# Moving 66 element-wise instructions of a Fourier and gated-MLP kernel from POOL to VectorE

## Chip, core and metric

One core of a Trainium2 chip runs the whole program. The metric is the device time of one execution in microseconds. PE is the matrix engine (TensorE), DVE is VectorE, ACT is ScalarE, POOL is GpSimd and SP the engine that issues the loads; each engine works through a queue of its own.

## What is computed

Three layers follow each other on 4 batches of 768 tokens with 384 channels, all in float32 at the inputs and outputs:

```
state = state + beta * outer(k_n, v - state^T k_n)   # 8 heads of 48, token by token
x  = concat of the heads' q @ state                  # [4, 768, 384]
u  = x + real(fft(fft(x, tokens), channels))
x2 = u + relu(norm(u) @ w_ch1) @ w_ch2               # 384 -> 1536 -> 384
h  = relu(x2 @ w_in)                                 # 384 -> 1024 = (hu, hv)
out = (hu * (w_spatial @ norm(hv) + b_spatial)) @ w_out
```

## The kernel before

**Attention (up to about 318 us).** The recurrence is done in chunks of 64 tokens, 12 chunks for each batch, four batches staggered. In each iteration PE runs four small stages; DVE subtracts, masks and scales (L384, L357); ACT copies out of the matmul banks. The order on every engine is written out by hand here: `chain()` ties each instruction behind the one before it on its engine. In the last 11 iterations other work is mixed in: the Fourier transform of batch 0 (`dft`) and the first five weight pieces (`conv2` in `tail()`).

**Fourier transform (`dft`).** One generator for each batch. Real input lets it fold the tokens on DVE (L575 to L586), form sums and differences of three parts (L591 to L596), then multiply by cosine and sine tables on PE (L603 to L609, L625), and add the result to x (L635 to L647). Batch 0 runs inside the attention, batches 1 to 3 inside the first MLP. In batch 0 the four additions into x are on DVE, in batches 1 to 3 on POOL.

**Weight pieces (`conv2`).** A matrix product of float32 quality is made of three passes in a reduced format: high by high, high by low, low by high (`PASS`). Each weight is therefore split into a high and a low part. For a piece of 128 by 384 (w1, w2, w_out) or 128 by 512 (w_in) the chain is: ACT scales the upper word (L678), DVE masks and merges the two 32-bit words of the 64-bit input in three instructions (L680, L681, L684), ACT rounds the result to the high part (L690), and POOL subtracts it from the result, which gives the low part (L691). The w_spatial pieces are float32 already and need only the ACT and the POOL step. The staging tile `cvd` has three buffers, which come free when the low part is written. There are 24 pieces of w1 and w2, 10 of w_in and w_out, 12 of w_spatial.

**First MLP (`mlp1`, about 316 to 682 us).** Eight groups of 384 tokens; in each, 12 blocks of hidden channels. For a block PE does nine matmuls (L760), ACT takes the relu as high part `hh` (L765), DVE makes the low part `hl` (L766), and one block later PE does nine matmuls into the three outputs (L775). In group 0 the weights of a block are converted just ahead of its use. The norm and transpose of the next group (L727 to L740, L716, L717) and the Fourier work of batches 1 to 3 are mixed in, then the pieces of w_in and w_out. From here on the order on each engine isn't written by hand: a planner sets it, from assumed costs of the instructions and the engine that each is given, in program order among those ready.

**Second MLP (`mlp2`, from about 682 us).** For each batch: values and their norm (L829 to L846), gates (L854, L861), the mix over tokens (L868) and the output (L888). The 12 pieces of w_spatial are converted during batch 0. POOL makes the low parts of the values (L846) and of the gated product (L879).

Of the kernel before, what the change touches and what calls it, by code (L numbers as in the profile page):

```python
# [7 lines left out]
F32 = mybir.dt.float32  # L8
# [50 lines left out]
class Kernel:  # L59
# [509 lines left out]
    def dft(self, b, x, p):  # L569
        nc, sc, dc, sg = self.nc, self.sc, self.dc, self.sg  # L570
        X = x[b]
        ff = p(0, [128, 3, 388])
        for t in range(3):
            xs = p(3, [128, 2, DM])
            nc.vector.tensor_add(xs[:, 0], X[:, t], X[:, 3 + t])  # L575
            nc.vector.tensor_sub(xs[:, 1], X[:, t], X[:, 3 + t])
            f = p(6, [128, DM])
            nc.vector.tensor_copy(out=f[:, 0:193:192], in_=xs[:, 0, 0:193:192])
            nc.vector.tensor_add(f[:, 1:192], xs[:, 0, 1:192], xs[:, 0, 383:192:-1])
            nc.vector.tensor_sub(f[:, 193:384], xs[:, 1, 1:192], xs[:, 1, 383:192:-1])  # L580
            h = ff[:, t]
            nc.vector.tensor_copy(out=h[:, 96:289:192], in_=f[:, 96:289:192])
            nc.vector.tensor_add(h[:, 0:96], f[:, 0:96], f[:, 192:96:-1])
            nc.vector.tensor_sub(h[:, 97:193], f[:, 0:96], f[:, 192:96:-1])
            nc.vector.tensor_add(h[:, 193:288], f[:, 193:288], f[:, 383:288:-1])
            nc.vector.tensor_sub(h[:, 289:384], f[:, 193:288], f[:, 383:288:-1])  # L586
            yield
        e0, e1, e2 = (ff[:, t, :DM] for t in range(3))
        ab = p(1, [128, 3, DM])
        sm, r3, c15 = (ab[:, t] for t in range(3))  # L590
        nc.gpsimd.tensor_add(sm, e1, e2)  # L591
        nc.vector.tensor_sub(e1, e1, e2)
        nc.gpsimd.tensor_add(e2, e0, sm)
        nc.vector.scalar_tensor_tensor(out=r3, in0=e0, scalar=sg[:, 0:1], in1=e1, op0=MUL, op1=SUB)
        nc.vector.scalar_tensor_tensor(out=c15, in0=e0, scalar=sg[:, 1:2], in1=e1, op0=MUL, op1=ADD)
        nc.vector.scalar_tensor_tensor(out=e0, in0=e0, scalar=2.0, in1=sm, op0=MUL, op1=SUB)  # L596
        yield
        z = []
        for g, (a0, a1) in enumerate(MG):
            m, o, n0 = a1 - a0, (0 if g < 2 else 641), (65 if g < 2 else 64)  # L600
            pz = self.bank("pf", [128, 512])
            zv = pz[:m, :384].rearrange("p (k r) -> p r k", r=6)
            nc.tensor.matmul(pz[:m, 0 : 6 * n0 : 6], lhsT=e2[:, a0:a1], rhs=sc[:, o : o + n0], start=True, stop=True)  # L603
            o += n0
            nc.tensor.matmul(zv[:, 3], lhsT=r3[:, a0:a1], rhs=sc[:, o : o + 64], start=True, stop=True)
            o += 64
            for r, w in ((slice(1, 6, 4), (c15, sm)), (slice(2, 5, 2), (e0, e1))):
                for i in range(2):
                    nc.tensor.matmul(zv[:, r], lhsT=w[i][:, a0:a1], rhs=sc[:, o : o + 128], start=(i == 0), stop=(i == 1))  # L609
                    o += 128  # L610
            if g % 2 == 0:
                z2 = p(4 + g // 2, [97, 2, 386])
            zz = z2[:, g % 2]
            n = 385 if g < 2 else 384
            nc.scalar.copy(out=zz[:m, :n], in_=pz[:m, :n])
            z.append(zz)
            yield
        A = p(0, [128, 3, 388]).rearrange("p t (a l) -> p t a l", a=2)

        def dst(out, k0, k1, gs):  # L620
            for g in gs:
                m = MG[g][1] - MG[g][0]
                lo, n = ((0, 97), (1, 96), (1, 96), (0, 97))[g]
                o = (0, 97, 193, 289)[g]
                nc.tensor.matmul(  # L625
                    out[:, lo : lo + 2 * n - 1 : 2], lhsT=z[g][:m, k0:k1], rhs=dc[:m, o : o + n], start=True, stop=True
                )

        for t in range(3):
            pf = self.bank("pf", [128, 2, 256])  # L630
            dst(pf[:, 1], 128 * t, 128 * t + 128, (2, 3))
            dst(pf[:, 0], 128 * t, 128 * t + 128, (0, 1))
            q = p(7, [128, 194])
            nc.scalar.copy(out=q[:, :193], in_=pf[:, 1, :193])
            nc.vector.tensor_sub(A[:, t, 0, :193], pf[:, 0, :193], q[:, :193])  # L635
            nc.vector.tensor_add(A[:, t, 1, :193], pf[:, 0, :193], q[:, :193])
            yield
        pf = self.bank("pf", [128, 2, 256])
        dst(pf[:1, 0], 384, 385, (0, 1))
        sv = p(8, [1, DM])  # L640
        nc.vector.tensor_add(sv[:, :193], X[0:1, 3, :193], pf[0:1, 0, :193])
        nc.vector.tensor_add(sv[:, 193:], X[0:1, 3, 193:], pf[0:1, 0, 191:0:-1])
        for e, lo in ((0, 0), (1, 1)):
            Y = X[:, 3 * e : 3 * e + 3]
            eng = nc.gpsimd if b else nc.vector
            eng.tensor_add(Y[:, :, :193], Y[:, :, :193], A[:, :, lo, :193])
            eng.tensor_add(Y[:, :, 193:], Y[:, :, 193:], A[:, :, 1 - lo, 191:0:-1])  # L647
        nc.gpsimd.tensor_copy(out=X[0:1, 3], in_=sv)
        self.mixed.add(b)
        yield  # L650

# [14 lines left out]
    def conv2(self, stg, w):  # L666

        nc = self.nc
        _, _, raw, src, n, new = w
        d = stg.tile([128, CK], F32, name="cvd", bufs=CF["cvd"])[:, :n]  # L670
        if raw is None:
            self.load(out=d, in_=src)
        else:
            r = raw.rearrange("p (n t) -> p n t", t=2)
            e = stg.tile([128, CK], I32, name="cve", bufs=CF["cve"])[:, :n]
            di = d.bitcast(I32)

            nc.scalar.activation(d, r[:, :, 1].bitcast(F32), AF.Abs, scale=2.0**-112)  # L678
            yield
            nc.vector.tensor_single_scalar(out=e, in_=r[:, :, 1], scalar=-(2**31), op=ALU.bitwise_and)  # L680
            nc.vector.scalar_tensor_tensor(  # L681
                out=di, in0=di, scalar=3, in1=e, op0=ALU.logical_shift_left, op1=ALU.bitwise_or
            )
            nc.vector.scalar_tensor_tensor(  # L684
                out=di, in0=r[:, :, 0], scalar=29, in1=di, op0=ALU.logical_shift_right, op1=ALU.bitwise_or
            )
        yield
        t = new(F32R)
        w[:2] = t[:, 0], t[:, 1]
        nc.scalar.copy(out=t[:, 0], in_=d)  # L690
        nc.gpsimd.tensor_sub(t[:, 1], d, t[:, 0].bitcast(F32))  # L691

    def weight(self, p, name, n, first=None):

# [431 lines left out]
```

## Time and profile before

| | |
|---|---|
| median of 3 runs | 945.8 us (944.82 to 946.86) |
| the profiled execution | 946.22 us, its span in the trace 944.4 us |
| PE busy | 890.4 us, 94% of the span |
| DVE busy | 580.0 us, 61% |
| ACT busy | 405.8 us, 43% |
| POOL busy | 155.1 us, 16%, 145 instructions |
| mean granted clock of PE | 0.969 of full speed |

The span runs from the first instruction to the last in the trace; the time of an execution holds a little more around it. A busy share is an average over stages with different limits, so it says little by itself: a stage is read from the stretch of the trace that holds it. The number before an arrow is what waits, the one behind it what released it.

### The profile page before, as it was taken

What the parts mean: (1) busy time and instruction counts of PE and PEld (TensorE: products, weight loads), DVE (VectorE), ACT (ScalarE), POOL (GpSimd) and SP (SyncE); (2) the same over time, 40 slices, a digit from 0 to 9 for tenths busy, and PEclk for the clock granted to TensorE, in tenths of its full rate; (3) what the DMA queues carried; (4) which work ended last, traced back from release to release, by engine and by line L of the source; (5) the groups of instructions that cost most, each with busy time, mean ns of one, the idle gap of its engine ahead of it and who ended that gap; (6) DMA issues with size and microseconds to landing.
All of it is one profiled execution on the core that took longest, in us unless ns stands there. A gap on an engine that the chain in (4) does not pass through costs nothing.

```text
span 944.4 us, 18349 instructions
## 1 busy us (share of the span) xinstructions
PE 890.4 (94%) x7232; PEld 846.2 (90%) x7232; DVE 580.0 (61%) x1678; ACT 405.8 (43%) x1030; POOL 155.1 (16%) x145
## 2 busy tenths in 40 slices
PE   7979899999898859999999999999999999999998
PEld 7569889988898748999998999999989999899898
DVE  5999999998876999375469422322372442533521
ACT  3367878898955435222225111111251342332421
POOL 2000000000001245212126000000072132132221
PEclk8968998999999879999999999999999999999999
DMA  8666576733262620000150000000020000000001
GB/s 237 174 177 167 145 185 183 191 104 86 78 190 68 236 83 1 1 1 1 40 163 0 1 1 1 1 1 17 26 76 26 26 1 26 26 1 26 26 1 51
DMA packets 51160, 67.13 MB, mean 71 GB/s; under 512 B 28897, under 2 KB 41410, under 8 KB 51074
## 3 DMA queue, kind: packets, MB, share of 16 engines
q1 hardware_dynamic: 51074, 65.96, 24.4%
q8 instruction: 57, 0.93, 0.4%
q14 instruction: 29, 0.24, 0.1%
HBM read 61.22 MB, written 4.72 MB: 70 GB/s over the span
## 4 chain that ended last, share of the span: by engine, by line
PE 66%; DVE 23%; ACT 4%; issue 2%; DMA 2%; POOL 2%; ACTq 0%; SPq 0%; POOLq 0%; DVEq 0%
PE bankY L775 13%; PE bankX L760 12%; PE bankX L868 11%; PE bankY L888 5%; PE bankX L854 5%; PE bankX L829 4%; DVE tm L273 4%; DVE Ts L278 4%; DVE cvd L681 2%; PE bankY L383 2%; PE bankY L367 2%; PE bankY L398 2%; PE bankY L396 2%; PE bankX L198 2%; PE bankX L609 2%
## 5 line engine op out<-in xcount | busy, mean ns | idle before, releaser
L760 PE MATMUL bankX<-uh,w 128*128 128x384 f32 x576 | 165.1, 348 | 12.6 <-ACT w L690 9.1
L775 PE MATMUL bankY<-w,hh 128*128 128x384 f32 x576 | 136.4, 343 | 1.2 <-ACT hh L765 0.4
L766 DVE SCALAR_TENSOR_TENSOR hl<-bankX,hh 128x384 fp32r<-128x384 f32 x96 | 52.9, 554 | 129.2 <-ACT hh L765 120.6
L765 ACT ACTIVATE hh<-bankX 128x384 fp32r<-128x384 f32 x96 | 46.6, 491 | 176.6 <-PE bankX L760 168.1
L760 PEld LDWEIGHTS bankX<-uh,w 128*128 128x128 f32 x576 | 106.5, 191 | 16.8 <-ACT w L690 11.1
L775 PEld LDWEIGHTS bankY<-w,hh 128*128 128x128 f32 x576 | 104.1, 190 | 4.2 <-POOL w L691 1.8
L868 PE MATMUL bankX<-ws,vh 128*128 128x384 f32 x384 | 98.6, 337 | 0.0
L760 PE MATMUL bankX<-ul,w 128*128 128x384 f32 x288 | 98.3, 341 | 0.0
L775 PE MATMUL bankY<-w,hl 128*128 128x384 f32 x288 | 83.6, 342 | 2.4 <-DVE hl L766 2.3
L876 DVE TENSOR_TENSOR g<-bankX,bsb 128x384 f32<-128x384 f32 x32 | 17.8, 557 | 102.0 <-PE bankX L868 102.0
L398 PE MATMUL bankY<-Sb,cw 112*112 112x96 f32 (+1 forms) x352 | 65.5, 269 | 11.3 <-DVE cw L384 8.9
L396 PE MATMUL bankY<-WU,gak 128*112 128x96 f32 (+1 forms) x384 | 69.6, 270 | 0.3
L868 PEld LDWEIGHTS bankX<-ws,vh 128*128 128x128 f32 x384 | 69.1, 188 | 0.0
L868 PE MATMUL bankX<-ws,vl 128*128 128x384 f32 x192 | 64.3, 337 | 0.0
L398 PEld LDWEIGHTS bankY<-Sb,cw 112*112 112x112 f32 (+1 forms) x352 | 49.4, 179 | 13.1 <-DVE cw L384 7.6
L278 DVE TENSOR_TENSOR Ts<-Ts,tm 128x110 f32<-128x110 f32 (+26 forms) x264 | 59.0, 261 | 0.8
L273 DVE TENSOR_TENSOR tm<-Ts 128x110 f32<-128x110 f32 (+26 forms) x264 | 58.9, 260 | 0.9
L367 PE MATMUL bankY<-gak,TT 128*128 128x96 f32 x384 | 55.2, 290 | 3.7 <-issue 3.1
L775 PEld LDWEIGHTS bankY<-w,hl 128*128 128x128 f32 x288 | 52.9, 189 | 4.4 <-DVE hl L766 4.3
L760 PEld LDWEIGHTS bankX<-ul,w 128*128 128x128 f32 x288 | 55.0, 191 | 0.2 <-DVE ul L717 0.2
L367 PEld LDWEIGHTS bankY<-gak,TT 128*128 128x128 f32 x384 | 49.9, 203 | 5.7 <-issue 3.3
L396 PEld LDWEIGHTS bankY<-WU,gak 128*112 128x112 f32 (+1 forms) x384 | 53.6, 182 | 1.0 <-ACT x L413 0.6
(168 smaller groups left out, 1853.1 us busy)
## 6 DMA issues: line engine op xcount, KB each, us to landing
kq<-in_kq_dram SPq DMA_DIRECT2D x40, 448.0 KB, 4.3
qt<-in_qt_dram SPq DMA_DIRECT2D x48, 196.0 KB, 3.7
gak<-in_kv_dram SPq DMA_DIRECT2D x48, 192.0 KB, 3.9
w<-in_w_dram SPq DMA_DIRECT2D x24, 384.0 KB, 7.3
out_dram<-ot SPq DMA_DIRECT2D x24, 192.0 KB, 2.0
kn<-in_kn_dram SPq DMA_DIRECT2D x16, 192.0 KB, 4.6
s<-in_wi_dram SPq DMA_DIRECT2D x6, 512.0 KB, 4.0
cvd<-in_ws_dram SPq DMA_DIRECT2D x12, 192.0 KB, 2.4
```

Of the source, the lines that this page charges most:

```text
L273: nc.vector.tensor_tensor(out=tm, in0=T[:, r, k : k + 1].to_broadcast(sh), in1=T[:, k : k + 1, :k].to_broadcast(sh), op=MUL)
L278: nc.vector.tensor_add(o, o, tm)
L367: nc.tensor.matmul(pb[:, hp].rearrange("p t d -> p (t d)"), lhsT=tt[:, o + hp], rhs=kv[:, hp], start=True, stop=True)
L396: nc.tensor.matmul(pd[:m, hp], lhsT=ak[:, hp, :m], rhs=u[:, hp], start=True, stop=(c == 0))
L398: nc.tensor.matmul(pd[:m, hp], lhsT=cw[:, hp, :m], rhs=sb[:, hp], start=False, stop=True)
L760: nc.tensor.matmul(ph, lhsT=w1[f][i][:, c * 128 : c * 128 + 128], rhs=cur[k][:, c], start=(c + j == 0), stop=(c == 2 and j == 2))
L765: nc.scalar.activation(hh, ph, AF.Relu)
L766: nc.vector.scalar_tensor_tensor(out=hl, in0=ph, scalar=0.0, in1=hh.bitcast(F32), op0=MAX, op1=SUB)
L775: nc.tensor.matmul(acc[t], lhsT=hx[i][:, t * 128 : t * 128 + 128], rhs=w2[e][k], start=(e == 0 and j == 0), stop=(e == 11 and j == 2),)
L854: nc.tensor.matmul(pu, lhsT=wi[2 * c][i][:, f * 128 : f * 128 + 128], rhs=xT[hf][k][:, c], start=(c + j == 0), stop=(c == 2 and j == 2),)
L868: nc.tensor.matmul(pv, lhsT=vn[i][:, s, f * 128 : f * 128 + 128], rhs=ws[2 * s + hf][k], start=(s + j == 0), stop=(s == 5 and j == 2),)
L888: nc.tensor.matmul(po, lhsT=gt[i][:, f, t * 128 : t * 128 + 128], rhs=wo[f][k], start=(f + j == 0), stop=(f == 3 and j == 2),)
```

## The change

The low parts of all weights (46 instructions), the sums of the Fourier transform (8 instructions, L591 and L593 for four batches), its additions into x for batches 1 to 3 (12 instructions) and its copy of one row into x (4 instructions) go from POOL to DVE. That the 4 additions of batch 0 were on DVE already leaves 66 instructions with 128 partitions and 4 one-row copies that move. POOL keeps the memsets, L846 and L879.

```
@@ dft
-        nc.gpsimd.tensor_add(sm, e1, e2)
+        nc.vector.tensor_add(sm, e1, e2)
         nc.vector.tensor_sub(e1, e1, e2)
-        nc.gpsimd.tensor_add(e2, e0, sm)
+        nc.vector.tensor_add(e2, e0, sm)
...
         for e, lo in ((0, 0), (1, 1)):
             Y = X[:, 3 * e : 3 * e + 3]
-            eng = nc.gpsimd if b else nc.vector
-            eng.tensor_add(Y[:, :, :193], Y[:, :, :193], A[:, :, lo, :193])
-            eng.tensor_add(Y[:, :, 193:], Y[:, :, 193:], A[:, :, 1 - lo, 191:0:-1])
-        nc.gpsimd.tensor_copy(out=X[0:1, 3], in_=sv)
+            nc.vector.tensor_add(Y[:, :, :193], Y[:, :, :193], A[:, :, lo, :193])
+            nc.vector.tensor_add(Y[:, :, 193:], Y[:, :, 193:], A[:, :, 1 - lo, 191:0:-1])
+        nc.vector.tensor_copy(out=X[0:1, 3], in_=sv)
@@ conv2
         nc.scalar.copy(out=t[:, 0], in_=d)
-        nc.gpsimd.tensor_sub(t[:, 1], d, t[:, 0].bitcast(F32))
+        nc.vector.tensor_sub(t[:, 1], d, t[:, 0].bitcast(F32))
```

## Rows read from the trace of the kernel before

**Rows 1.** The chain that ended last, shares of the span by engine.

```profile
PE 66%; DVE 23%; ACT 4%; issue 2%; DMA 2%; POOL 2%; ACTq 0%; SPq 0%; POOLq 0%; DVEq 0%
```

**Rows 2.** Busy time by stretch: length, PE, PEld, DVE, ACT, POOL, clock, DMA, GB/s.

```profile
296.00:318.00 22.00, 17.78 (x132) 16.52 (x132) 20.07 (x44) 12.28 (x31) 4.52 (x5) 0.84 0.13 30
318.00:345.00 27.00, 19.84 (x85) 15.73 (x85) 27.00 (x75) 10.14 (x21) 12.26 (x9) 0.91 0.66 254
345.00:378.00 33.00, 25.99 (x123) 22.51 (x123) 31.03 (x53) 14.97 (x32) 15.74 (x14) 0.87 0.00 1
378.00:480.00 102.00, 100.64 (x663) 99.31 (x662) 53.64 (x170) 23.15 (x54) 16.94 (x15) 1.00 0.06 20
480.00:520.00 40.00, 37.94 (x222) 36.35 (x221) 35.62 (x70) 18.16 (x37) 20.40 (x15) 1.00 0.22 70
...
680.00:712.00 32.00, 30.99 (x161) 27.93 (x161) 22.60 (x62) 17.43 (x42) 20.12 (x18) 1.00 0.19 56
```

**Rows 3.** Waits of PE, 318 to 378 us: total us, times, longest.

```profile
PE bankX L760 <- ACT w L690: 9.1, 6, 3.1
PE bankX L760 <- POOL w L691: 3.4, 3, 1.7
```

**Rows 4.** POOL's groups, 296 to 378 us: busy us, mean ns, idle before.

```profile
L691 POOL TENSOR_TENSOR w<-cvd,w 128x384 fp32r<-128x384 f32 x24 | 28.8, 1205 | 58.9 <-ACT w L690 47.2 <-DMA w<-in_w_dram 11.7
```

**Rows 5.** DVE's groups, 296 to 378 us.

```profile
L681 DVE SCALAR_TENSOR_TENSOR cvd<-cvd,cve 128x384 int32<-128x384 int32 x23 | 19.2, 840 | 1.8 <-ACT cvd L678 1.5
L684 DVE SCALAR_TENSOR_TENSOR cvd<-w,cvd 128x384 int32<-128x384 int32 x23 | 14.9, 648 | 0.2
L680 DVE TENSOR_SCALAR cve<-w 128x384 int32<-128x384 int32 x23 | 11.0, 477 | 0.0
L766 DVE SCALAR_TENSOR_TENSOR hl<-bankX,hh 128x384 fp32r<-128x384 f32 x11 | 6.0, 545 | 0.0
...
L717 DVE TENSOR_TENSOR ul<-bankX,uh 128x384 fp32r<-128x384 f32 x5 | 2.7, 548 | 0.4 <-ACT uh L716 0.4
...
L711 DVE TENSOR_SCALAR l1v<-l1v 128x3 f32<-128x3 f32 x2 | 1.9, 931 | 0.0
...
L578 DVE COPY s<-s 128x2 f32<-128x2 f32 x4 | 1.8, 439 | 0.0
```

**Rows 6.** Single lines over the whole span: ns min/median/max, first and last start.

```profile
L681 DVE SCALAR_TENSOR_TENSOR cvd<-cvd,cve x34: 544/560/1789, 289.0 to 516.5; 128x384 int32<-128x384 int32 x28, 128x512 int32<-128x512 int32 x6
L684 DVE SCALAR_TENSOR_TENSOR cvd<-w,cvd x24: 530/552/1386, 289.6 to 376.6; 128x384 int32<-128x384 int32 x24
L680 DVE TENSOR_SCALAR cve<-w x24: 326/348/1194, 288.5 to 372.3; 128x384 int32<-128x384 int32 x24
L711 DVE TENSOR_SCALAR l1v<-l1v x8: 129/168/991, 309.8 to 526.1; 128x3 f32<-128x3 f32 x8
L578 DVE COPY s<-s x12: 146/159/996, 264.9 to 450.7; 128x2 f32<-128x2 f32 x12
```

**Rows 7.** DVE in order of time: start, us, line.

```profile
325.43 0.55 DVE L576 TENSOR_TENSOR s<-x 128x384 f32<-128x384 f32 x1
325.90 0.55 DVE L684 SCALAR_TENSOR_TENSOR cvd<-w,cvd 128x384 int32<-128x384 int32 x1
```

**Rows 8.** ACT's copies to the high part: ns min/median/max, first and last start.

```profile
L690 ACT CAST w<-cvd x24: 494/512/517, 296.4 to 377.2; 128x384 fp32r<-128x384 f32 x24
```

**Rows 9.** Waits, 385 to 480 us.

```profile
PE bankX L603 <- POOL s L593: 1.4, 1, 1.4
```

**Rows 10.** Waits, 480 to 522 us.

```profile
PE bankY L775 <- DVE hl L766: 2.0, 2, 1.6
```

**Rows 11.** The additions into x on either engine: ns min/median/max.

```profile
L646 POOL TENSOR_TENSOR x<-x,s x6: 1202/1315/1443, 396.7 to 486.8; 128x579 f32<-128x579 f32 x6
L646 DVE TENSOR_TENSOR x<-x,s x2: 744/745/746, 300.6 to 302.0; 128x579 f32<-128x579 f32 x2
```

## The prediction

> **What bounds the kernel now.** I read the chain of waits first, to see which engines set the end: PE holds 66% of it, DVE 23%, POOL 2% [rows 1]. So POOL's own time is hardly on the path, and DVE's is. Then I cut the span into stretches around the instructions that move [rows 2]. Three kinds of stage show. From 296 to 378 us DVE is the bound: 20.07 of 22 us, 27.00 of 27 and 31.03 of 33, while PE is busy for 17.78, 19.84 and 25.99 us. This is the end of attention and group 0 of the first MLP, where each weight must be converted before its matmuls. From 378 us on PE is full (100.64 of 102, 37.94 of 40, 30.99 of 32) and DVE has slack, except from 480 to 520 us, where it is busy for 35.62 of 40 us with the pieces of w_in and w_out. Before 296 us nothing but one pair of Fourier sums is touched.
>
> The waits of PE from 318 to 378 us say what the first stage lacks: 9.1 us for ACT's high parts and 3.4 us for POOL's low parts [rows 3]. ACT is busy for 10.14 of 27 and 14.97 of 33 us [rows 2], so it isn't slow; it waits for DVE, which feeds it. What shortens DVE's work between 296 and 378 us shortens the kernel, and what lengthens it there lengthens the kernel.
>
> **What POOL costs DVE now.** The 24 low parts take POOL 28.8 us, 1.205 us each [rows 4], beside the work of DVE. It isn't free. In the same stretch lines of DVE take longer than they usually do: L681 has a mean of 840 ns against a median of 560 over the whole span, L684 648 against 552, L680 477 against 348, and tiny ones stretch most: L711, on 3 elements, 931 against 168, L578, on 2 elements, 439 against 159 [rows 5, 6]. The lines that read one operand from a matmul bank, L766 and L717, keep 545 and 548 ns [rows 5]. So an instruction of DVE that works on SBUF alone is held while POOL works, and others aren't. The time lost, mean less median, by count: L681 23 x 0.28 = 6.4 us, L684 23 x 0.096 = 2.2, L680 23 x 0.129 = 3.0, L711 2 x 0.763 = 1.5, L578 4 x 0.28 = 1.1. Three more small lines (L580, L709, L710) repeat L711's pattern, one long use of about 0.8 us each, 2.4 in all. That makes 16.6 us over 27 instructions of POOL, 0.61 us each. And once DVE stands idle for 1.5 us before L681, until ACT has written a staging tile [rows 5]; ACT waited there for the tile to come free, that is for POOL.
>
> **What the same work costs on DVE.** The trace has no low part of a weight on DVE, but L717 and L766 are the same subtraction with the same result type, at 545 to 548 ns, and L576 with both inputs in SBUF takes 0.55 us [rows 5, 7]. In a full queue the next instruction starts earlier: L576 starts at 325.43 and L684 behind it at 325.90, so each takes 0.47 us of the queue [rows 7]. Between 296 and 378 us there come 24 low parts, two Fourier sums of batch 1 and one copy of a row. At 0.47 us the 26 are 12.2 us; for the copy I take 0.3, between L578's 0.16 and the 0.47. Together 12.5 us.
>
> Balance on DVE in this stretch: -16.6 - 1.5 + 12.5 = -5.6 us. Bounds: if the stretching had another cause and stayed, +12.5 - 1.5 = +11, which would be a slower kernel and is counted with the first rival below; that the waits of 3-element lines grow fivefold only beside POOL speaks against it. If the low parts fill gaps as well, -7.
>
> **The wait that is added.** A low part needs ACT's high part, a copy of 0.512 us [rows 8], and now DVE itself stands in line for it, with the next piece, `hl` and the norm queued behind. From below the cost is nothing, if other work stands between L684 and the subtraction; from above it is 24 x 0.51 = 12.2 us. The nearest rows are L717 and L766, which wait for ACT in just this way: 0.4 us over 16 instructions, 0.025 each [rows 5]. I take that: 24 x 0.025 = +0.6. The order is set by a planner that puts an instruction in the queue when its inputs should be there, which speaks for the low end; in the attention's last iterations (4 of the 24) the order is written out, and ACT's copy stands just ahead of the subtraction in the same step.
>
> **The other places.**
> - Fourier sums of batch 2: PE waits 1.4 us for L593 [rows 9], which takes POOL 1.3. On DVE it is 0.55, so I take -0.8 (bounds -1.4 and 0). The other batches' sums are waited for by nobody on PE.
> - Pieces of w_in and w_out, 480 to 520 us: PE loses 2.0 us to `hl` behind DVE's full queue [rows 10]. By the same 0.61 us, the 10 low parts cost DVE 6.1 us now and 6 x 0.6 + 4 x 0.47 = 5.5 then, where 0.6 is 0.47 scaled by 512/384. Little changes: I take -0.5 (bounds -2 and +1).
> - Additions into x, batches 1 to 3: 1.315 us on POOL, 0.745 on DVE [rows 11]. Four in a row now hold DVE for 3.0 us, with `hl` behind them, while PE is full [rows 2] and no cover is left if `hl` is late. PE has another block's nine matmuls between, so I take +0.5 (bounds 0 and +3, one microsecond for each batch). The loads into the slots of the last batch's tables start 2 us earlier, which nothing waits for.
> - w_spatial, 680 to 712 us: 12 x 0.47 = 5.6 us on a DVE that is idle for 9.4 of 32 [rows 2], against 12 x 0.61 = 7.3 of stretching gone. PE loses 1.0 us there now. I take 0 (bounds -1 and +1).
> - Batch 0's sums, before 296 us: DVE has room there and PE is not held by them; 0.
>
> **Sum.** -5.6 + 0.6 - 0.8 - 0.5 + 0.5 = -5.8 us. The profiled execution took 946.2 us for a span of 944.4, so it would be 940.4; against the median of 945.8, 0.4 lower, the forecast is **940.0 us**. Its own range is 937 to 943.5.
>
> **Rivals.**
> - *DVE waits for ACT (slower).* In its single queue DVE stands before each low part until the copy is through. What speaks for it: all 24 pieces run L684, copy, subtraction, and no independent work is promised between. Against it: 0.025 us for each of 16 like instructions. It decides from 5.6 / 24 = 0.23 us per low part on; fully exposed it is 12.2 - 5.6 = +6.6, or 952.4. Chance 0.16.
> - *A new order (no change).* The planner plans with other engines and may put PE's blocks in another order after 378 us, where PE is full and every hole shows. Three holes of the size of [rows 9, 10], 1.5 us each, give back 4.5 of 5.8: 944.5. That the gain has no place to go otherwise speaks against it. Chance 0.14.
> - *No overlap on DVE.* A subtraction released by a semaphore may take its whole 0.55 us instead of 0.47: 26 x 0.08 = 2.1 us less gain, 942.1. [Rows 7] speak against it in a full queue. Chance 0.10. The Trainium skill has this as a rule (VectorE: DVE Perf Modes, The DRAIN you can't avoid): the next instruction starts only when the pipeline of the one before is empty. By the same page (The TRN2 errata) an estimate is (384 + 151) / 0.96 = 557 ns each, with which the sum would be -3.5 us; the trace agrees on the duration and not on the spacing.
> - *PE no longer waits for weights.* Both waits of [rows 3] go, 12.5 us, and 0.8 of the Fourier sums: 932.5. DVE would have to shed twice what I count. Chance 0.10.
>
> **Numbers.** The forecast has 0.50. Faster by over 0.2% (1.9 us, about what a measurement of this kernel can tell from no change): forecast, no overlap and no waits, 0.70. Same 0.14, slower 0.16. Range 932 to 948.5: it takes in all but the far end of the first rival and the tail below the last, some 0.15.
>
> **What would show it.** Right: L681, L684, L680, L711 near their medians between 296 and 378 us; L691 on DVE at 0.55 us; the last w piece some 5 us earlier; less waiting of L760. Wrong: idle time of DVE before L691 released by L690 above 0.23 us each; the stretching still there without POOL; new holes of PE after group 0, at L775 for `hl` or at L603.

## The result and the profile after

The changed kernel takes 937.02 us (median, 936.13 to 937.29), beside 946.33 us of the kernel before on the same chip: a ratio of 0.9905 [0.9894, 0.9917]. So it is faster, as forecast, and inside the range of 932 to 948.5, but the gain of 9.3 us is 1.6 times the forecast 5.8. The profiled execution took 936.92 us for a span of 935.1. Behind L645 every line number is now one lower: the high part is L689, the low part L690, the matmuls of the first MLP L759 and L774.

First the page, its busy times and the shares of the chain that ended last:

```profile
PE 884.8 (95%) x7232; PEld 842.7 (90%) x7232; DVE 579.9 (62%) x1748; ACT 405.3 (43%) x1030; POOL 70.3 (8%) x75
...
PE 72%; DVE 20%; ACT 5%; issue 2%; DMA 1%; POOL 0%; ACTq 0%; DVEq 0%; POOLq 0%
```

DVE was given 70 instructions and is busy for 579.9 us, where it was 580.0 before. What it took over it got back by working faster. PE's share of the chain went from 66% [rows 1] to 72%, DVE's from 23% to 20%.

The same stretches as in [rows 2]; the one from 345 us is also cut where the weights now end, at 372:

```profile
296.00:318.00 22.00, 16.54 (x122) 14.96 (x122) 19.41 (x49) 12.04 (x30) 0.00 (x0) 0.84 0.16 43
318.00:345.00 27.00, 19.11 (x88) 15.45 (x86) 27.00 (x87) 9.63 (x21) 0.00 (x0) 0.94 0.63 244
...
345.00:378.00 33.00, 30.78 (x165) 28.37 (x166) 28.38 (x66) 16.82 (x36) 0.00 (x0) 0.90 0.00 0
372.00:378.00 6.00, 6.00 (x38) 5.96 (x37) 1.55 (x4) 1.46 (x3) 0.00 (x0) 1.00 0.00 0
378.00:480.00 102.00, 99.62 (x653) 98.14 (x653) 60.96 (x194) 22.18 (x53) 0.00 (x0) 1.00 0.08 25
480.00:520.00 40.00, 40.00 (x234) 39.62 (x233) 36.17 (x90) 17.94 (x37) 0.00 (x0) 1.00 0.18 57
680.00:712.00 32.00, 32.00 (x175) 30.41 (x174) 18.39 (x65) 15.01 (x34) 10.80 (x9) 1.00 0.14 43
```

From 318 to 345 us DVE is still full, but it gets through 87 instructions where it got through 75. From 372 us on it is nearly free and PE is full: group 0 ends some 6 us earlier. In the two later stretches PE, which lost 2.06 us of 40 and 1.01 of 32, now loses nothing. Only from 378 to 480 us is PE worse off: 99.62 us where it had 100.64.

DVE's groups from 296 to 378 us, against [rows 5, 6]:

```profile
L690 DVE TENSOR_TENSOR w<-cvd,w 128x384 fp32r<-128x384 f32 x24 | 12.9, 550 | 0.2 <-ACT w L689 0.2
L683 DVE SCALAR_TENSOR_TENSOR cvd<-w,cvd 128x384 int32<-128x384 int32 x23 | 12.7, 551 | 0.1
L680 DVE SCALAR_TENSOR_TENSOR cvd<-cvd,cve 128x384 int32<-128x384 int32 x23 | 12.4, 550 | 0.1
L679 DVE TENSOR_SCALAR cve<-w 128x384 int32<-128x384 int32 x23 | 8.1, 352 | 0.0
...
L578 DVE COPY s<-s 128x2 f32<-128x2 f32 x4 | 0.6, 150 | 0.0
...
L710 DVE TENSOR_SCALAR l1v<-l1v 128x3 f32<-128x3 f32 x2 | 0.3, 165 | 0.0
```

Every mean is at the median that the line had over the whole span before. The 840 ns are 550, the 931 ns of three elements are 165. And the 24 low parts made DVE wait for ACT for 0.2 us in all. Their end, in DVE's order of time (start, us, line):

```profile
370.55 0.55 DVE L683 SCALAR_TENSOR_TENSOR cvd<-w,cvd 128x384 int32<-128x384 int32 x1
371.01 0.55 DVE L690 TENSOR_TENSOR w<-cvd,w 128x384 fp32r<-128x384 f32 x1
371.73 0.56 DVE L690 TENSOR_TENSOR w<-cvd,w 128x384 fp32r<-128x384 f32 x1 [0.17 <-ACT w L689]
```

A low part starts 0.46 us behind the instruction ahead of it, though each lasts 0.55. The last one starts at 371.73 us; on POOL it started at 377.81:

```profile
377.81 1.02 POOL L691 TENSOR_TENSOR w<-cvd,w 128x384 fp32r<-128x384 f32 x1 [1.69 <-ACT w L690]
```

PE's waits from 318 to 378 us, and then those from 378 us to the end:

```profile
PE bankX L759 <- ACT w L689: 4.7, 4, 1.9
PE bankX L759 <- DVE w L690: 3.6, 2, 1.9
PE bankY L774 <- DVE w L690: 1.5, 1, 1.5
PE bankY L774 <- ACT w L689: 0.2, 1, 0.2
```

```profile
PE bankX L739 <- DVE un L731: 2.4, 1, 2.4
```

Of the 12.5 us that L760 waited [rows 3] its successor L759 still waits 8.3, and L774 waits 1.7: this stage is still bound by the weights. The waits of [rows 9, 10] are gone, and a new one has come, for the norm `un`.

To place the 9.3 us, the start of the n-th matmul of the changed kernel is compared with that of the kernel before (7232 in each trace, one profiled execution of each). The table gives the change in that difference over five parts of the span, in us; the times are those of the kernel before. It also holds the kernels of the next section.

```
                     0-283   283-409   409-497   497-543   691-720   whole
changed kernel       -0.84     -5.09     +0.94     -2.95     -1.35    -9.27
w1w2_only            -0.97     -5.98      0.00     +0.47     -0.04    -6.51
win_wout_only        -1.74     +0.03     -0.02     -2.97     +0.02    -4.69
wspatial_only        -1.03     +1.13      0.00     +0.04     -1.28    -1.14
fourier_only         -1.17     -2.48     +2.51     -1.33     +0.05    -2.42
weights_only         -0.42     -6.26     -0.01     -2.98     -1.30   -10.97
weights_only_again   -0.96     -6.25     -0.02     -2.98     -1.45   -11.66
additions_on_pool    -1.51     -6.36     +1.20     -2.98     -1.43   -11.08
sums_on_pool         -0.59     -4.29     +3.69     -2.91     -1.40    -5.48
all_on_vector        -0.71     -5.08     +0.94     -2.95     -1.50    -9.26
ghost_read           -0.51     +4.06     +2.56     -1.96     -1.25    +2.92
ghost_write          -1.00     -4.90     +2.41     -2.91     -1.28    -7.66
```

Before 283 us nothing differs but batch 0's pair of Fourier sums, and all 12 gain 0.4 to 1.7 us there, those that leave the sums alone too: the profiled execution of the kernel before was slow in its attention. That is a spread of single executions and no effect of the change; `wspatial_only` has 1.13 us more in a stretch where it differs in nothing. What is under some 1.2 us in this table is read only where it repeats.

A part of this spread is PE's granted clock. From 283 to 409 us it stood at half (1.2 of 2.4 GHz) for 20.5 us in the kernel before, for 17.1 in the changed kernel and in all kernels that move the pieces of w1 and w2 and give POOL no useless work, for 27.3 in `wspatial_only` and for only 10.2 in `fourier_only`. So the -2.48 of `fourier_only` isn't read as an effect of its edit. How much of the other gains the 3.4 us less at half hold, at most about 1.7 (an estimate: half of 3.4), was not separated.

### The profile page after: what moved, and what is told of

It reads as the page before. It is cut to its first block, busy times and chain, and to the rows that moved or that the text cites. A ratio compares the mean times of both kernels' runs of the same rounds, so it can differ in the third digit from the quotient of the medians.

```text
span 935.1 us, 18282 instructions
## 1 busy us (share of the span) xinstructions
PE 884.8 (95%) x7232; PEld 842.7 (90%) x7232; DVE 579.9 (62%) x1748; ACT 405.3 (43%) x1030; POOL 70.3 (8%) x75
## 4 chain that ended last, share of the span: by engine, by line
PE 72%; DVE 20%; ACT 5%; issue 2%; DMA 1%; POOL 0%; ACTq 0%; DVEq 0%; POOLq 0%
PE bankX L759 14%; PE bankY L774 14%; PE bankX L867 11%; PE bankX L853 5%; PE bankX L828 5%; PE bankY L887 5%; DVE tm L273 4%; DVE Ts L278 4%; PE bankY L383 2%; PE bankY L367 2%; PE bankY L396 2%; PE bankY L398 2%; PE bankX L609 2%; PE bankX L198 1%; DVE cw L384 1%
## 5 line engine op out<-in xcount | busy, mean ns | idle before, releaser
L759 PE MATMUL bankX<-uh,w 128*128 128x384 f32 x576 | 163.9, 347 | 8.3 <-ACT w L689 4.7
L774 PE MATMUL bankY<-w,hh 128*128 128x384 f32 x576 | 136.6, 343 | 1.8 <-DVE w L690 1.5
L759 PEld LDWEIGHTS bankX<-uh,w 128*128 128x128 f32 x576 | 106.5, 191 | 12.1 <-ACT w L689 6.4
L774 PEld LDWEIGHTS bankY<-w,hh 128*128 128x128 f32 x576 | 103.6, 190 | 4.2 <-DVE w L690 2.3
L759 PE MATMUL bankX<-ul,w 128*128 128x384 f32 x288 | 97.9, 340 | 0.0
L774 PE MATMUL bankY<-w,hl 128*128 128x384 f32 x288 | 82.2, 340 | 0.0
L845 POOL TENSOR_TENSOR vl<-v,vh 128x512 fp32r<-128x512 f32 x24 | 31.7, 1328 | 531.0 <-DMA cvd<-in_ws_dram 457.4
L759 PEld LDWEIGHTS bankX<-ul,w 128*128 128x128 f32 x288 | 55.0, 191 | 0.0
L774 PEld LDWEIGHTS bankY<-w,hl 128*128 128x128 f32 x288 | 53.2, 189 | 0.4 <-DVE hl L765 0.3
```

The costliest lines, as they stand in the source:

```text
L759: nc.tensor.matmul(ph, lhsT=w1[f][i][:, c * 128 : c * 128 + 128], rhs=cur[k][:, c], start=(c + j == 0), stop=(c == 2 and j == 2))
L774: nc.tensor.matmul(acc[t], lhsT=hx[i][:, t * 128 : t * 128 + 128], rhs=w2[e][k], start=(e == 0 and j == 0), stop=(e == 11 and j == 2),)
```

## Experiments

**The parts, each alone.** Four kernels move one part each; everything else is as before.

```
+    def conv2(self, stg, w, low):
...
-        nc.gpsimd.tensor_sub(t[:, 1], d, t[:, 0].bitcast(F32))
+        low.tensor_sub(t[:, 1], d, t[:, 0].bitcast(F32))
```

Here `low` is VectorE for the 24 pieces of w1 and w2, for the 10 of w_in and w_out, or for the 12 of w_spatial, and GpSimd for the others. The fourth kernel is the changed one with this line on GpSimd.

> Only the 24 low parts of w1 and w2 are on VectorE; all else as before. If VectorE's time in group 0 decides, by the 0.61 us that one POOL subtraction takes from it against 0.47 us for its own, this part gives about 5 us: 941.3 us, with group 0's last weight about 5 us earlier. If the planner's new order or run-to-run spread made most of the 9 us, it gives under 2 us: 944 or more.

> Only the 10 low parts of w_in and w_out are on VectorE. The prediction priced them at -0.5 us: 945.8. Matched matmul by matmul, the two traces show 2.9 us won between 505 and 521 us: if that belongs to these ten alone, 943.4; if it needs the earlier additions into x too, in between.

> Only the 12 low parts of w_spatial are on VectorE. The prediction priced them at 0: 946.3. The traces show 1.35 us won between 696 and 707 us, where TensorE no longer waits 1.0 us: if these twelve did it, 945.0.

> Only the Fourier sums, the additions into x and the row copies are on VectorE; all weights' low parts on POOL as before. The prediction priced this at -0.3 us: 946.0. The traces show a loss of 0.9 us near 410 us, where the norm of the next group comes late behind the sums: 947.2 if it belongs to this part alone.

| kernel | median us | ratio to before |
|---|---|---|
| w1w2_only | 939.85 | 0.9935 [0.9923, 0.9948] |
| win_wout_only | 942.25 | 0.9965 [0.9952, 0.9977] |
| wspatial_only | 944.81 | 0.9988 [0.9979, 0.9996] |
| fourier_only | 945.66 | 0.9997 [0.9988, 1.0005] |

Beside 945.9 us of the kernel before these are -6.05, -3.65, -1.1 and -0.2 us, -11.0 together, where the whole gave 9.3. So the three groups of weights, 10.8 us together, give more than the change does. That points to a cost of the Fourier part when it comes on top; the kernels further down look at that.

The 10 pieces of w_in and w_out are worth 3.65 us where the forecast had 0.5. Why shows in DVE's groups from 480 to 520 us, first of the kernel before, then of the changed one:

```profile
L681 DVE SCALAR_TENSOR_TENSOR cvd<-cvd,cve 128x512 int32<-128x512 int32 x6 | 6.1, 1048 | 0.0
...
L684 DVE SCALAR_TENSOR_TENSOR cvd<-s,cvd 128x512 int32<-128x512 int32 x6 | 4.7, 787 | 0.0
L681 DVE SCALAR_TENSOR_TENSOR cvd<-cvd,cve 128x384 int32<-128x384 int32 x4 | 4.0, 1028 | 0.0
L680 DVE TENSOR_SCALAR cve<-s 128x512 int32<-128x512 int32 x6 | 3.5, 604 | 1.4 <-DMA s<-in_wi_dram 1.4
```

```profile
L683 DVE SCALAR_TENSOR_TENSOR cvd<-s,cvd 128x512 int32<-128x512 int32 x6 | 4.1, 683 | 0.0
L690 DVE TENSOR_TENSOR s<-cvd,s 128x512 fp32r<-128x512 f32 x6 | 4.0, 682 | 0.0
L680 DVE SCALAR_TENSOR_TENSOR cvd<-cvd,cve 128x512 int32<-128x512 int32 x6 | 4.0, 681 | 0.0
...
L679 DVE TENSOR_SCALAR cve<-s 128x512 int32<-128x512 int32 x6 | 2.4, 420 | 1.1 <-DMA s<-in_wi_dram 1.1
...
L680 DVE SCALAR_TENSOR_TENSOR cvd<-cvd,cve 128x384 int32<-128x384 int32 x4 | 2.1, 551 | 0.0
```

The two shapes of L681 alone lost 6 x 0.367 + 4 x 0.477 = 4.1 us, with the other steps (mean of before less mean of after, by count) 7.2, or 0.72 for each low part on POOL, where the forecast took 0.61. And the hole of PE there was larger than [rows 10] say. The waits of PE's weight loads in the kernel before, from 480 to 522 us, and then from 670 to 720 us:

```profile
PEld bankY L775 <- DVE hl L766: 3.0, 3, 1.9
```

```profile
PEld bankX L854 <- ACT uT L861: 1.3, 1, 1.3
```

The table's -2.97 and -1.28 are these 3.0 and 1.3: the whole hole closed in both places, and in the traces of the kernels that move these weights neither wait is left above 0.2 us. `fourier_only` closes part of the first hole too (-1.33): its trace still waits 1.7 us of the 3.0 there. One hole can't be won twice, which is one reason why the parts don't add up.

**Does POOL's reading hold DVE, or was it POOL's slowness?** The rival of the contention is the chain's length: POOL took 1.2 us for a low part and kept a staging tile for it. Two kernels keep the changed program and give POOL useless work for each of the 34 raw pieces. In the first it reads the finished high part and writes a scratch tile that nobody reads; no staging tile waits for that.

```
         nc.vector.tensor_sub(t[:, 1], d, t[:, 0].bitcast(F32))
+        if raw is not None:
+            gh = stg.tile([128, CK], mybir.dt.bfloat16, name="gho")
+            nc.gpsimd.tensor_sub(gh[:, :n], t[:, 0].bitcast(F32), t[:, 0].bitcast(F32))
```

> The changed kernel, and for each of the 34 pieces of w1, w2, w_in and w_out POOL also subtracts the high part from itself into a scratch tile that nobody reads, where its old subtraction stood; outputs are as before. If POOL holds VectorE while both work, the 0.61 us of each comes back on top: 24 x 0.61 = 14.6 us in group 0 and some 3 to 5 us at w_in and w_out, 952 to 957 us. If the gain came from the low parts being ready sooner and the staging tile free sooner, nothing comes back: 937.

In the second POOL reads a single column and then writes the scratch tile four times:

```
+            nc.gpsimd.tensor_copy(out=gh[:, :1], in_=t[:, 0, :1].bitcast(F32))
+            for _ in range(4):
+                nc.gpsimd.memset(gh, 0.0)
```

> As the run with the scratch subtraction, but POOL copies one column of the high part and then sets the scratch tile to zero four times: it writes and hardly reads. If any work of POOL holds VectorE, the time comes near that run's. If only what both engines read collides, VectorE's instructions with two inputs are free and at most the third of the lost time that fell on one-input lines (L679, L710, L578: 5.6 of 16.6 us) comes back: 937 to 942 us.

The first takes 948.93 us, 1.0033 [1.0021, 1.0045] of the kernel before: 11.9 us of useless reads cost more than the change had won. The second takes 939.43 us, 0.9935 [0.9918, 0.9951], 2.4 more than the changed kernel. DVE's groups of the reading kernel from 296 to 390 us, with POOL's own:

```profile
L690 DVE TENSOR_TENSOR w<-cvd,w 128x384 fp32r<-128x384 f32 x24 | 17.1, 722 | 0.2 <-ACT w L689 0.2
L680 DVE SCALAR_TENSOR_TENSOR cvd<-cvd,cve 128x384 int32<-128x384 int32 x23 | 15.2, 669 | 0.1
...
L768 DVE SCALAR_TENSOR_TENSOR hl<-bankX,hh 128x384 fp32r<-128x384 f32 x13 | 7.1, 548 | 2.7 <-ACT hh L767 2.7
...
L594 DVE SCALAR_TENSOR_TENSOR s<-s,sg 128x384 f32<-128x384 f32 x1 | 1.2, 1180 | 0.0
...
L693 POOL TENSOR_TENSOR gho<-w 128x384 bf16<-128x384 f32 x24 | 29.7, 1238 | 127.9 <-ACT w L689 127.4
```

And of the writing kernel:

```profile
L690 DVE TENSOR_TENSOR w<-cvd,w 128x384 fp32r<-128x384 f32 x24 | 12.9, 546 | 0.2 <-ACT w L689 0.2
...
L680 DVE SCALAR_TENSOR_TENSOR cvd<-cvd,cve 128x384 int32<-128x384 int32 x23 | 12.4, 547 | 0.1
...
L736 DVE TENSOR_SCALAR un<-x,mv,l1r 128x384 f32<-128x384 f32 x6 | 3.6, 661 | 0.0
...
L695 POOL MEMSET gho<- 128x512 bf16 x93 | 50.1, 539 | 5.4
```

With 29.7 us of reading on POOL two of the three steps with two operands in SBUF (the on-chip memory beside the matmul banks) stretch again, 722 and 669 ns against 550; one with an operand in a matmul bank doesn't (548). The third such step, L683, has a mean of 571 against 551: only 4 of its 23 begin while POOL reads, where 9 of 24 low parts do. With 50.1 us of memsets the two stay at 546 and 547. What stretches beside memsets are some lines with one large or tiny operand in SBUF: `un` 661 against 474, a line on 3 elements 290 against 165, and from 480 to 520 us L679 with 384 columns 598 against 354. So for steps with two operands it is the reading that collides, and the contention is shown: the time is lost again though no staging tile hangs on POOL. The rival, which expected no loss, falls. The size was overrated: 948.93 lies under the 952 to 957 us that the contention was given. The stretching of the lines from 296 to 390 us sums to some 11 us over 24 reads, 0.46 each, against 0.61 for the low parts before.

The Trainium skill has both halves as a rule (SBUF — State Buffer, Who interferes with whom): an instruction of VectorE with two inputs in SBUF contends with one of GpSimd that reads SBUF, and not with one that only writes it, while instructions in a two-port mode contend with either. The two traces agree: 722 and 669 ns beside reads, 546 and 547 beside writes.

**The Fourier part on top.** All 46 low parts of weights on VectorE, the Fourier part as before; and the changed kernel with the low parts of the second MLP (L845, L878) on VectorE as well, which leaves POOL only the memsets.

```
# weights_only, against before
-        nc.gpsimd.tensor_sub(t[:, 1], d, t[:, 0].bitcast(F32))
+        nc.vector.tensor_sub(t[:, 1], d, t[:, 0].bitcast(F32))
# all_on_vector, against the changed kernel
-                nc.gpsimd.tensor_sub(vn[1][:, t], v, vn[0][:, t].bitcast(F32))
+                nc.vector.tensor_sub(vn[1][:, t], v, vn[0][:, t].bitcast(F32))
...
-                    nc.gpsimd.tensor_sub(gt[1][:, f], g, gt[0][:, f].bitcast(F32))
+                    nc.vector.tensor_sub(gt[1][:, f], g, gt[0][:, f].bitcast(F32))
```

> All 46 low parts of weights on VectorE, the Fourier sums, additions and row copies on POOL as before. The three parts alone gave 6.1, 3.3 and 1.1 us, 10.5 in all, and the Fourier part 0.2. If parts add, 935.6, below the changed kernel by 1.4; if they share a gain, as the 9.0 us of the whole against 10.7 of its parts suggest, 937.

> The changed kernel with the second MLP's low parts of values and of the gated product on VectorE as well, so that POOL has only memsets. VectorE is busy for 82 of 223 us there and TensorE is full, so no gain is due but at the end, where the last low part takes 1.02 us on POOL and would take 0.55: 936.5. If the low parts make the norm's chain late, 938 to 940.

`weights_only` takes 935.48 us, 0.9887 [0.9872, 0.9901]: no worse than the changed kernel, and 1.5 us below it. `all_on_vector` takes 937.25 us, 0.9907 [0.9892, 0.9922], and its row of the table is that of the changed kernel: from 712 us on PE is busy for 218.98 of 223.10 us in the changed kernel, and what is moved there doesn't reach the end. The 936.5 us expected for it didn't come.

Which half of the Fourier part would cost the 1.5 us? The changed kernel with the sums on POOL, or with the additions and the row copies on POOL:

```
# sums_on_pool
-        nc.vector.tensor_add(sm, e1, e2)
+        nc.gpsimd.tensor_add(sm, e1, e2)
...
-        nc.vector.tensor_add(e2, e0, sm)
+        nc.gpsimd.tensor_add(e2, e0, sm)
# additions_on_pool: the three lines in the loop over e as before the change
```

> The changed kernel, but the sums L591 and L593 stay on POOL; the additions into x and the row copies are on DVE, and so are all low parts of weights. Theory one, the sums cost the time: with L591, L593 in DVE's queue just ahead of the norm's steps (405.7 to 409.5 us), PE waited 2.4 us for `un` (L731), where the kernel with the weights alone waited 1.4 for L593; without them it should wait for L593 at most 1.4 again and come out near the kernel with the weights alone, 935.0 to 936.0. Rival, the additions cost it (12 at 0.745 us on DVE, ahead of `hl` and the norm): then this kernel stays at 936.7 to 937.5 and the wait for `un` stays. If the order of the planner alone decides, any place between, with another wait of PE at 400 to 412 us.

> The mirror of the one before: the sums L591 and L593 on DVE, the additions into x of batches 1 to 3 and the row copies on POOL, all low parts of weights on DVE. Theory one (the sums cost it): 936.7 to 937.5 and PE's wait of about 2.4 us for `un` L731 near 408 us is there. Rival (the additions cost it): 935.0 to 936.0 and no such wait. The 12 additions on POOL read SBUF beside DVE for 15.8 us in all; the collision they bring is on stretches where PE is full, so it should cost nothing by either.

> All 46 low parts of weights on DVE, the Fourier part as before the change, run again beside the other two: 935.5, and below the changed kernel (937.0) by 1 to 2 us if moving the Fourier part really gives time back; within 0.5 us of it if the first look was chance.

They take 940.17 us, 0.9933 [0.9918, 0.9948]; 937.1 us, 0.9903 [0.9886, 0.992]; and 935.19 us, 0.9886 [0.987, 0.9901]. `weights_only` repeats, now 1.8 us below the changed kernel. The intervals still touch that of the changed kernel, but each of the 8 executions with the weights alone (934.50 to 936.11 us) lies below each of the 4 of the changed kernel and the 4 of `all_on_vector` (936.13 to 937.58): a cost of the Fourier part is likely, and its size stays open. Neither half fits its theory. Without the sums the kernel should have come back to 935 to 936 or stayed at 937, and it got slower. With the additions on POOL it has the time that the first theory told, but not the wait for `un` that was to cause it. What each has is another wait of PE around 405 to 412 us, here of `weights_only_again`, `additions_on_pool` and `sums_on_pool` in turn:

```profile
PE bankX L603 <- POOL s L593: 1.4, 1, 1.4
```

```profile
PE bankX L603 <- DVE s L593: 2.6, 1, 2.6
```

```profile
PE bankX L739 <- DVE un L731: 3.6, 1, 3.6
```

The table's part from 409 to 497 us follows these waits: 1.4 us goes with 0.0, the changed kernel's 2.4 with +0.94, 2.6 with +1.20. By the same count the 3.6 us of `sums_on_pool` would be +2.2, and they are +3.69. The rest goes with PE's clock: behind that wait it was granted at half for 3.4 us. The changed kernel's wait of 2.4 us stands in four more traces. In `all_on_vector` the clock stayed full behind it, as in the changed kernel (+0.94 in both); in `fourier_only`, `ghost_read` and `ghost_write` it fell to half for 3.4 us, and the stretch costs +2.51, +2.56 and +2.41. In columns as in [rows 2], from 408 to 416 us, the changed kernel and then `ghost_write`:

```profile
408.00:412.00 4.00, 2.00 (x14) 2.01 (x15) 3.84 (x11) 0.00 (x0) 0.00 (x0) 1.00 0.01 4
412.00:416.00 4.00, 4.00 (x34) 3.99 (x33) 1.02 (x2) 1.87 (x4) 0.00 (x0) 1.00 0.00 0
```

```profile
408.00:412.00 4.00, 1.98 (x9) 1.98 (x10) 3.87 (x11) 0.00 (x0) 0.00 (x0) 0.73 0.02 4
412.00:416.00 4.00, 4.00 (x30) 3.99 (x29) 1.02 (x2) 1.28 (x3) 0.00 (x0) 0.84 0.00 0
```

The hole is the same (2.00 and 1.98 us of 4 busy), and some 9 matmuls fewer are begun or finished in these 8 us. So a hole of PE here costs its length, and some 1.5 us more when the clock falls behind it; why it fell in some traces and not in others isn't shown. The times don't follow from these holes alone: the four profiled executions took 934.5, 936.9, 935.1 and 940.7 us for holes of 1.4, 2.4, 2.6 and 3.6, and what is left lies in group 0 (below). The cause of the changed kernel's wait is where the planner puts the norm in DVE's queue. In `weights_only` and in the changed kernel:

```profile
403.16 1.95 DVE L732 TENSOR_SCALAR un<-x,mv,l1r 128x384 f32<-128x384 f32 x3
```

```profile
408.47 0.55 DVE L593 TENSOR_TENSOR s<-s,s 128x384 f32<-128x384 f32 x1
408.94 0.61 DVE L594 SCALAR_TENSOR_TENSOR s<-s,sg 128x384 f32<-128x384 f32 x1
409.47 1.25 DVE L731 TENSOR_SCALAR un<-x,mv,l1r 128x384 f32<-128x384 f32 x3
```

The same three steps of the norm run 6 us later, behind the Fourier sums, while PE has run out of work. That the order costs the time is what the waits show; that another order with the sums on DVE would win it back was not tried.

Of group 0 a difference stays open. With the additions on POOL, as in both `weights_only` kernels and `additions_on_pool`, the part from 283 to 409 us gains 6.3 to 6.4 us, with them on DVE 5.1 (the changed kernel, `all_on_vector`) or 4.3 (`sums_on_pool`). It isn't the additions' own time, since the first one that is moved starts at 391 us, nor the planner's order alone: compared as in the table, from 283 to 318 us, before the planned part, the first three gain 0.9 to 1.0 us and the last three lose 1.1. There, at the end of the attention, PE waits in the changed kernel

```profile
PE bankY L383 <- ACT WU L372: 1.9, 1, 1.9
```

and as long in `all_on_vector` and `sums_on_pool`, but only 0.7 us in `additions_on_pool` and not at all in the `weights_only` kernels. The clock's first fall behind 283 us lies elsewhere too, from about 310 to 317 us in those with the long wait and from 304 to 312 in the others. What brings the two about no run here tells; the row copy of batch 0 on DVE is not enough, since `ghost_write` has it too and doesn't have the wait.

## Why the prediction was right, and what it mis-sized

The forecast by its terms, against the changed kernel's row of the table:

- *The conversion stretch, -5.6 + 0.6 = -5.0.* Measured -5.09. On DVE its working holds point by point: the lines stand at their medians, a low part is 0.55 us long and takes 0.46 to 0.47 of the queue, and the last one starts 6.1 us earlier, 5.2 of it won behind 283 us. Only the added wait was smaller, 0.2 us over 24 instead of 0.6. That POOL's reading was the cause is shown by the two kernels with useless work. That the table comes within 0.1 us is partly luck: it adds +1.1 up to 318 us and -6.2 behind, the kernels that move the same weights lie between -4.29 and -6.36, and the clock, 3.4 us less at half, had no term.
- *w_in and w_out, -0.5.* Measured -2.95: the term that was mis-sized most. Two steps failed. The stretching was carried over from the other stage at 0.61 us each, where the rows of this stage give 0.72. And the gain was read from DVE's balance and bounded at 2 by PE's own waits, though PE had lost 2.06 of 40 us [rows 2] to one late engine: where PE is the bound, what can be won is its hole. The weight loads' wait of 3.0 us says how large it is.
- *w_spatial, 0.* Measured -1.35, beyond its bound of -1, for the same reason: the wait of 1.3 us at the weight loads went, whole. The term set stretching against new work on an engine that had slack, and so found nothing.
- *Fourier sums and additions, -0.8 + 0.5 = -0.3.* Measured +0.94, a wrong sign. The wait for L593 went, as forecast, and a wait of 2.4 us for the norm took its place in the same queue. The forecast put the delay on `hl`; it fell on `un`. No term allowed for the clock behind such a hole, which the profiled execution was spared.
- *Not forecast:* -0.84 before 283 us, a slow attention in the one execution from which the sum was made.

So the forecast has the main mechanism right and comes out too small mainly by two terms on PE's holes.

One reading was too broad: that an instruction of DVE on SBUF alone is held while POOL works. In the kernel before, 11 of the 23 L681 from 296 to 378 us begin while POOL works, and last 1156 ns on average where the other 12 last 551. But L579 and L583, on SBUF alone too, keep 344 and 246 ns (2 each) where they begin beside POOL.

The rivals. *DVE waits for ACT* fell: 0.008 us for each low part, where it decides from 0.23 on. *No overlap on DVE* fell on the spacing of 0.46 us. *PE no longer waits for weights* fell, since 10.0 us are still waited for weights; its time of 932.5 was missed by only 4.5 us because holes closed elsewhere. *A new order* was half right: at one hole it came, and `sums_on_pool` shows that it can cost 3.7 us there, 1.5 of them with the clock. The parts that the forecast undervalued (-3.8 us in two places) outweighed it.

## What to carry to other kernels

Before an element-wise instruction is given to an idle engine, look at what its neighbours' instructions last beside it and apart from it: means far over the median of the same line, above all on tiny operands, are the price. Then take each stage by what bounds it: where PE is the bound, the gain is PE's hole (read it at the weight loads as well, and look at the clock behind it), and where DVE is, its balance. If a planner orders the queues, move the part that pays and leave the rest: here the weights alone took 935.2 to 935.5 us, and the Fourier part on top brought nothing or a loss of 1.5 to 1.8.

## What the hardware showed unexpectedly

POOL seems to be held as well, not only DVE. In the writing kernel its one-column copy, with nothing else changed, starts twice 2.7 us apart:

```profile
326.40 0.32 POOL L693 CAST gho<-w 128x1 bf16<-128x1 f32 x1 [7.03 <-ACT w L689]
326.78 2.27 POOL L695 MEMSET gho<- 128x512 bf16 x4
329.11 2.18 POOL L693 CAST gho<-w 128x1 bf16<-128x1 f32 x1
```

It lasts 0.32 us and then 2.18 for the same 128 numbers, beside a DVE that works without a gap; over 24 of them the mean is 914 ns. Spans on POOL are rough, and what on DVE would hold it was not isolated. And memsets aren't free for every line of DVE: beside 50.1 us of them six `un` were 187 ns longer each. That this made the kernel 2.4 us slower is not shown: its hole at `un` near 408 us is 2.4 us long as in the changed kernel, and the 1.5 us that it loses more from 409 to 497 us (+2.41 against +0.94) go with the clock that fell behind that hole.
